# Kept rows stored later, fewer kept combinations, and the first tile's end inside the third stage of a four-layer kernel

## The chip, the cores and the metric

The kernel runs on one core of a Trainium2 chip. The metric is the device time of one execution, in microseconds (us); a run's time is the time of that core.

## What is computed

Four layers act on x of 2048 rows by 640 columns, in float32, each adding its result to x after a layer norm:

```python
x = x + _A_ref(_layernorm(x), A_wqkv, A_wo)
x = x + _B_ref(_layernorm(x), ...)
x = x + _A_ref(_layernorm(x), A_wqkv, A_wo)
x = x + _B_ref(_layernorm(x), ...)
# A: attention, 32 heads of 20, each row sees 8 rows at distances 0, 2, ... 14
# B: a = x @ dft_hid_re.T ; b = x @ dft_hid_im.T
#    y = dft_seq_re @ a - dft_seq_im @ b
```

The change lies in layers B. They are numbered 1 and 3 in the code (`self.li`).

## The kernel before

**Layer B.** Its rows, after the norm, stand in four SBUF tiles `self.xn[0..3]` (shown as `r1_0` to `r1_3`), four rows of blocks each, every value split into a high half and a low half so that three matmul passes of the rounded type give float32 precision (`PASSES`). The sequence matrices come from HBM in pieces of 128 x 512 (`cs_in`, 256 KB), which land in the buffers `win` (a ring of five) and `xa` (two). ScalarE (ACT) makes the high half of a piece and VectorE (DVE) the low half; such a pair is a split. Some pieces are first combined with one another by a DVE addition (line 1536 in layer 3, `combine`).

**Stages.** The eight output tiles are made in three steps. `z_mm` (line 1182) makes the sequence products of tiles 0 and 1 over 16 row blocks; `ymm` (line 1249) multiplies them by the hidden matrices and `yout` adds the old x and stores. Tiles 2 to 7 are then made in three pairs (`p` = 0, 1, 2), each pair in three sweeps (`sw`) of eight steps (`i`), by sums and differences of row blocks that need fewer products. These row combinations (`xc` in HBM) are made by `x_whole` and `x_combine` (line 1799) while `z_mm` still runs. Combination 3 is simply the plain rows, which `x_keep` (line 1299) stores, eight stores of 256 KB. Layer 1 runs the pairs by `pair` (line 1851), layer 3 by `pairs7` (line 1478), which also makes the hidden products with fewer multiplications: `v_stage` (line 1444) does one of eight stages of them for a tile, and needs sums of the hidden matrices (`wvb` in HBM), which `v_get` loads back, so many in each step as the table `GETS` says for each sweep of pair 0.

**Kept combinations.** In the third sweep of a pair, layer 1 forms b11 + b12 of two loaded pieces and stores the result in HBM (`ccb`, `keep`, line 1912, 24 stores of 256 KB); layer 3 loads it (`pre`, line 1511) in place of the plain piece, and so does no addition there.

**What sets the order.** All loads and stores of these stages are issued by SyncE (SP) in one queue. Instructions of each engine run in the order in which they are placed. In `run` (line 2015) only TensorE (PE) keeps the order of the code; the others are placed by a scheduler at build time, `x_keep` among them. In `pairs7` all engines but GpSimd (POOL) keep the order of the code. There, `load(n)` and `loadx(n)` fetch the pieces and row combinations of step n two steps ahead, `fifo` holds the splits to be made, and `fill` makes them as soon as one of six places is free (four in the columns 0 to 255 of `r1_2` and `r1_3`, and `s0`, `s1`); a place comes free when PE has used the half before it.

**The end of tile 1's sequence products.** After the last `z_mm` the five PSUM banks `m0`, `m1`, `xt`, `t0`, `t1` are emptied by `evac1` into `zo0`, `zo1`, `zo2` and `ot`. The first step of `pairs7` writes the same banks again: its first product m0 and m1, its second xt and t0, its third t1 and `pq`.

Of the kernel before, what the change touches and what calls it, by code (L numbers as in the profile page):

```python
# [10 lines left out]
F32 = mybir.dt.float32  # L11
# [139 lines left out]
NP = 8  # L151
# [17 lines left out]
    (2, ("a22", "t4"), (1, 0), (1, 0)),  # L169
    (3, None, (1, 1), (1, 1)),  # L170
)
GETS = ((0, 1, 1, 1, 1, 1, 1, 2), (2, 2, 1, 1, 1, 1, 1, 1), (0, 0, 1, 1, 1, 1, 1, 1))
NST = 16
FA = 64
GW = (512, 512, 512, 384)
SLOTS = NJ + W - 1
# [5 lines left out]
def tile_layers(ctx: ExitStack, tc: tile.TileContext, x, wqkv, wo, cs, cst, wre, wim, out):  # L182
# [897 lines left out]
    class LayerB:  # L1080
# [397 lines left out]
        def pairs7(self):  # L1478
# [32 lines left out]
            def pre(p, i):  # L1511
                tag, bufs = wide[self.nraw % len(wide)]
                self.nraw += 1
                raw = T([P, 2, 256], tag, bufs=bufs) if tag != "win" else wtile([P, 2, 256])
                nc.sync.dma_start(raw.rearrange("p r t -> p (r t)"), ccb[:, p, i])
                return raw

            def load(n):
                if n >= len(steps):
                    return  # L1520
                p, sw, i = steps[n]
                t1, t2 = 2 * p + 2, 2 * p + 3
                if sw == 0:
                    raws[n] = [self.s_raw(*a, wide) for a in ((t1, NP + i), (t1, i), (t2, NP + i))]
                elif sw == 1:
                    raws[n] = [self.s_raw(*a, wide) for a in ((t1, i), (t2, NP + i), (t1, NP + i))]
                else:
                    raws[n] = [self.s_raw(*a, wide) for a in ((t2, NP + i), (t2, i))] + [pre(p, i)]

            def loadx(n):  # L1530
                if n < len(steps):
# [11 lines left out]
            def atoms(n):  # L1543
# [31 lines left out]
                    combine(b22, b12, b22, ALU.subtract)  # L1575
                    half(n, "c3", b22)

                return [c0, lambda: half(n, "p12", raws[n][1]), lambda: half(n, "c6", raws[n][2])]

            fifo = []  # L1580
            held = [0]
# [31 lines left out]
                fifo += atoms(n)  # L1613
            for n in range(2):
                loadx(n)
            for n, (p, sw, i) in enumerate(steps):
                t1, t2 = 2 * p + 2, 2 * p + 3
                tp = t1 - 1
# [180 lines left out]
        def x_combine(self, m, i):  # L1799
            (ca, ka), (cb, kb), sign = XC[m]  # L1800
            op = ALU.add if sign > 0 else ALU.subtract
            va, vb = (self.whole[c][:, :, k * 256 : (k + 1) * 256] for c, k in ((ca, ka), (cb, kb)))
            self.nc_ += 1
            tag = CFG["xcr"][self.nc_ % len(CFG["xcr"])]
            hl = T([P, 2, 2, 256], tag, F32R, bufs=CFG["bufs"].get(tag, 2))
            hi, lo = hl[:, :, 0], hl[:, :, 1]
            nc.vector.tensor_tensor(lo.bitcast(F32), va, vb, op=op)
            nc.scalar.copy(hi, lo.bitcast(F32))
            nc.vector.tensor_tensor(lo, lo.bitcast(F32), hi.bitcast(F32), op=ALU.subtract)
            nc.sync.dma_start(self.xc[m][:, i : i + 2], hl.bitcast(F32))  # L1810

        def x_slot(self, m, i, slots):
            c, j = slots[self.nx % len(slots)]
# [37 lines left out]
        def pair(self, p, nstats, hooks=None):  # L1851
# [63 lines left out]
            def ahead_c(i):  # L1915
                b12, b22, b11 = raw(t2, i), raw(t2, NP + i), raw(t1, i)
                x6 = self.x_slot(6, i, ring)
                c3 = split(combine(b22, b12, b22, ALU.subtract))

                def rest():  # L1920
                    keep(i, combine(b11, b11, b12, ALU.add))
                    return split(b11)

                return x6, c3, split(b12), rest
# [90 lines left out]
        def run(self, nstats):  # L2015
# [6 lines left out]
            with ExitStack() as st:  # L2022
# [3 lines left out]
                for s in range(NST):  # L2026
# [4 lines left out]
                        if f"{t}{s}" not in self.done:  # L2031
                            fn()
                    self.z_mm(s, None, 1)
                    if self.seven and 4 <= s < 4 + NP:
                        self.x_keep(s - 4)
                    self.tick()
                    for h in range(2):
                        ks = [k for k in range(KD) if R["y"][h][k] == s]
# [6 lines left out]
                            fn, args = todo.pop(0)  # L2045
                            fn(*args)
                assert not todo
                if R["y"][1][4] == NST:
                    self.ymm(0, 1, R["y"][1].index(NST), KD)
                    self.yout(0, 1, nstats)  # L2050
                self.evac(1)
            if self.seven:
                with tc.manual_schedule(engines=ENGINES - {nc.gpsimd.engine}):
                    self.pairs7()
# [74 lines left out]
```

## Time and profile before

| what | value |
|---|---|
| three runs | 1736.44, 1732.24, 1733.15 us |
| their median | 1733.15 us |
| the profiled execution's own time | 1733.94 us |
| its span in the trace | 1732.2 us |
| busy time in the span | PE 1709.7, DVE 1383.2, ACT 830.6, POOL 615.2 us |
| granted PE clock | 1.0 throughout, that is the 2.4 GHz level |
| moved by DMA | 444.45 MB, 257 GB/s on average |

The span runs from the first to the last instruction; 1.7 us lie around it. Busy times of the engines overlap. Idle time of PE is what counts here, since PE is busy nearly throughout; an idle time of DVE or ACT costs only where PE waits for it in the end.

### The profile page before, as it was taken

What the parts mean: (1) busy time and instruction counts of PE and PEld (TensorE: products, weight loads), DVE (VectorE), ACT (ScalarE), POOL (GpSimd) and SP (SyncE); (2) the same over time, 40 slices, a digit from 0 to 9 for tenths busy, and PEclk for the clock granted to TensorE, in tenths of its full rate; (3) what the DMA queues carried; (4) which work ended last, traced back from release to release, by engine and by line L of the source; (5) the groups of instructions that cost most, each with busy time, mean ns of one, the idle gap of its engine ahead of it and who ended that gap; (6) DMA issues with size and microseconds to landing.
All of it is one profiled execution on the core that took longest, in us unless ns stands there. A gap on an engine that the chain in (4) does not pass through costs nothing.

```text
span 1732.2 us, 26800 instructions
## 1 busy us (share of the span) xinstructions
PE 1709.7 (99%) x8771; PEld 1487.6 (86%) x8771; DVE 1383.2 (80%) x2201; ACT 830.6 (48%) x1838; POOL 615.2 (36%) x570
## 2 busy tenths in 40 slices
PE   9999999999999999999999999999999999999999
PEld 7888887878888888888888889888888888888888
DVE  5999999978778767767739998899787668778775
ACT  5665645655455445445534444455543444444541
POOL 4899999940000000000019997899300000000000
PEclk9999999999999999999999999999999999999999
DMA  7877679959899788787658856799588988878872
GB/s 253 258 228 260 213 242 312 330 191 353 275 334 303 252 260 262 229 277 242 210 160 271 259 172 212 239 329 331 175 319 294 293 276 271 256 255 266 266 248 88
DMA packets 296059, 444.45 MB, mean 257 GB/s; under 512 B 32080, under 2 KB 171728, under 8 KB 295664
## 3 DMA queue, kind: packets, MB, share of 16 engines
q1 hardware_dynamic: 281744, 433.06, 75.3%
q10 hardware_dynamic: 14176, 9.67, 1.8%
q8 instruction: 70, 1.15, 0.3%
q14 instruction: 69, 0.57, 0.1%
HBM read 345.18 MB, written 97.46 MB: 256 GB/s over the span
## 4 chain that ended last, share of the span: by engine, by line
PE 82%; DVE 7%; DMA 5%; ACT 2%; issue 2%; POOL 2%; SPq 0%; ACTq 0%; DVEq 0%
PE m L513 19%; PE aux L1249 9%; PE aux L676 6%; PE t L1601 5%; PE m L1601 5%; PE m L1843 5%; PE t L1843 5%; PE aux L1465 5%; PE m L1182 4%; PE t L1182 4%; PE pq L1601 3%; PE pq L1843 3%; PE xt L1601 2%; PE xt L1843 2%; DMA win<-cs_in 2%
## 5 line engine op out<-in xcount | busy, mean ns | idle before, releaser
L513 PE MATMUL m<-r,s 128*128 128x512 f32 (+1 forms) x1890 | 421.8, 378 | 0.1
L513 PEld LDWEIGHTS m<-r,s 128*128 128x128 f32 x1890 | 344.6, 188 | 54.6 <-ACT sg L528 1.4
L593 DVE TENSOR_TENSOR pr<-pq,win 128x1280 f32<-128x1280 f32 x128 | 189.8, 1483 | 37.2 <-PE aux L1249 20.3
L651 POOL TENSOR_TENSOR pr<-pr 128x640 f32<-128x640 f32 x126 | 207.7, 1648 | 27.9 <-DVE pr L636 26.6
L596 POOL TENSOR_TENSOR pr<-pr 128x640 f32<-128x640 f32 x123 | 176.7, 1436 | 88.1 <-DVE pr L593 88.0
L636 DVE TENSOR_TENSOR pr<-pq,win 128x1280 f32<-128x1280 f32 x128 | 190.3, 1488 | 2.6
L314 POOL TENSOR_TENSOR stats<-stats,mhalf 128x1 f32<-128x1 f32 (+1 forms) x26 | 18.9, 728 | 448.7 <-ACT stats L308 448.7
L1249 PE MATMUL aux<-r2a,zo 128*128 128x320 f32 x480 | 141.4, 309 | 0.0
L1249 PE MATMUL aux<-pr,zo 128*128 128x320 f32 x440 | 130.1, 309 | 0.0
L652 POOL TENSOR_TENSOR pr<-pr 128x320 f32<-128x320 f32 x126 | 112.9, 896 | 9.9
L606 DVE TENSOR_REDUCE lg<-pr 128x64 f32<-128x640 f32 (+1 forms) x128 | 107.2, 837 | 11.5 <-POOL pr L596 11.2
L1836 ACT CAST r<-win 128x512 fp32r<-128x512 f32 x126 | 76.2, 618 | 75.8 <-DVE win L1872 54.7
L1182 PE MATMUL m<-s,r 128*128 128x512 f32 x348 | 106.9, 395 | 2.4 <-ACT r L1119 0.9
L1182 PE MATMUL t<-s,r 128*128 128x512 f32 x348 | 105.2, 390 | 0.0
L1540 ACT CAST r<-win 128x512 fp32r<-128x512 f32 x111 | 68.3, 621 | 75.4 <-DVE win L1536 34.8
L527 ACT COPY stg<-m 128x480 f32<-128x480 f32 x96 | 53.6, 558 | 94.2 <-PE m L513 88.2
L1837 DVE TENSOR_TENSOR r<-win,r 128x512 fp32r<-128x512 f32 x126 | 84.6, 688 | 16.7 <-ACT r L1836 16.1
L1541 DVE TENSOR_TENSOR r<-win,r 128x512 fp32r<-128x512 f32 x111 | 75.9, 689 | 23.1 <-ACT r L1540 22.9
L1249 PEld LDWEIGHTS aux<-r2a,zo 128*128 128x128 f32 x480 | 90.1, 188 | 1.4
L1249 PEld LDWEIGHTS aux<-pr,zo 128*128 128x128 f32 x440 | 82.6, 188 | 1.6
L676 PE MATMUL aux<-r2a,ot 128*128 128x320 f32 x540 | 83.7, 310 | 0.0
L676 PEld LDWEIGHTS aux<-r2a,ot 128*128 128x128 f32 x540 | 80.4, 188 | 1.5 <-ACT wa L499 0.3
(450 smaller groups left out, 3827.2 us busy)
## 6 DMA issues: line engine op xcount, KB each, us to landing
win<-cs_in SPq DMA_DIRECT2D x330, 256.0 KB
r<-xc SPq DMA_DIRECT2D x264, 256.0 KB
win<-kvb SPq DMA_DIRECT2D x96, 440.0 KB
xa<-cs_in SPq DMA_DIRECT2D x112, 256.0 KB
win<-kvb SPq DMA_DIRECT2D x64, 360.0 KB
xc<-sg SPq DMA_DIRECT2D x28, 512.0 KB
kvb<-stg SPq DMA_DIRECT2D x33, 320.0 KB
qs<-qb SPq DMA_DIRECT2D x64, 160.0 KB
```

Source lines behind the costliest of these rows:

```text
L513: nc.tensor.matmul(mt[g][:, : GW[q]], st[:, a, k], wq[q][:, b, k], start=n == 0, stop=n == 14)
L593: nc.vector.tensor_tensor(pr, q, wview(u, jp, 0, [[1, FE]]), op=ALU.mult)
L596: nc.gpsimd.tensor_tensor(pv[:, :, 0:10], pv[:, :, 0:10], pv[:, :, 10:20], op=ALU.add)
L606: nc.vector.tensor_reduce(rows(lgs[u], jp), pv.rearrange("p (a h) d -> p a h d", h=HE), axis=AX.X, op=ALU.add,)
L636: nc.vector.tensor_tensor(pr.rearrange("p j w (h d) -> p (j w) h d", d=DH), rows(lgs[u], jp).unsqueeze(3).to_broadcast([P, 2 * W, HE, DH]) ...
L651: g.tensor_tensor(pr[:, :, 0:4], pr[:, :, 0:4], pr[:, :, 4:8], op=ALU.add)
L652: g.tensor_tensor(pr[:, :, 0:2], pr[:, :, 0:2], pr[:, :, 2:4], op=ALU.add)
L676: nc.tensor.matmul(m[:, :320], oT[(c, j)][:, a, k], wo_s["w"][:, b, k, e * 320 : (e + 1) * 320], start=(i, k) == (0, 0), stop=(i, k) == (2 ...
L1182: self.last = nc.tensor.matmul(self.z[t][k], self.xn[c][:, a, j, k * P : (k + 1) * P], self.ct[s][:, b], start=s == 0 and i == 0, stop=s = ...
L1249: self.last = nc.tensor.matmul(self.ym[e][:, :320], zt[(k, a, ri)][:, j2 * P : (j2 + 1) * P], w[:, e * 320 : (e + 1) * 320], start=(k, a, ...
L1601: nc.tensor.matmul(bank, w(a, kb), h[b], start=start and (a, b) == (0, 0) and not cont, stop=stop and (a, b) == (1, 0), skip_group_check=cont,
L1843: nc.tensor.matmul(bank, w(a, kb), hl[b], start=start and (a, b) == (0, 0), stop=stop and (a, b) == (1, 0),)
```

## The change

Five things are done:

- Layer 1 no longer stores the combinations of pair 2 for steps 4 to 7 (`kept`), 4 stores of the 24. Layer 3 loads the plain piece for these steps and adds it itself on DVE.
- `x_keep` is called in the last eight rounds of `z_mm` in place of rounds 4 to 11, and each of its stores is put behind the last store of `x_combine` on SP (`issue_after`).
- In layer 3, the last `ymm`, the emptying of tile 1's banks and the last `yout` leave `run` and stand at the start of `pairs7`, behind the loads of the first two steps; a split is made ahead of the emptying and another behind the third bank. So DVE and ACT now keep the written order there.
- In `GETS`, the third sweep's loads of sums stand one step earlier each: counts 0, 1, 1, 1, 1, 1, 1, 0 in place of 0, 0, 1, 1, 1, 1, 1, 1.
- `keep` is split so that the addition is done in any case.

```diff
-GETS = ((0, 1, 1, 1, 1, 1, 1, 2), (2, 2, 1, 1, 1, 1, 1, 1), (0, 0, 1, 1, 1, 1, 1, 1))
+GETS = ((0, 1, 1, 1, 1, 1, 1, 2), (2, 2, 1, 1, 1, 1, 1, 1), (0, 1, 1, 1, 1, 1, 1, 0))
+def kept(p, i):
+    return p < NPAIR - 1 or i < NP // 2
...
-                    raws[n] = [self.s_raw(*a, wide) for a in ((t2, NP + i), (t2, i))] + [pre(p, i)]
+                    raws[n] = [self.s_raw(*a, wide) for a in ((t2, NP + i), (t2, i))]
+                    raws[n].append(pre(p, i) if kept(p, i) else self.s_raw(t1, i, wide))
...
-                return [c0, lambda: half(n, "p12", raws[n][1]), lambda: half(n, "c6", raws[n][2])]
+                def c2():
+                    _, b12, b11 = raws[n]
+                    if not kept(p, i):
+                        combine(b11, b11, b12, ALU.add)
+                    half(n, "c6", b11)
+
+                return [c0, lambda: half(n, "p12", raws[n][1]), c2]
...
             for n in range(2):
                 loadx(n)
+            if self.y1 < KD:
+                self.ymm(0, 1, self.y1, KD)
+            self.zt_new(1)
+            fill(1)
+            for k in range(KD):
+                self.evac1(1, k)
+                if k == 2:
+                    fill(1)
+            if self.y1 < KD:
+                self.yout(0, 1, None, 2)
...
-            nc.sync.dma_start(self.xc[m][:, i : i + 2], hl.bitcast(F32))
+            self.sdma = nc.sync.dma_start(self.xc[m][:, i : i + 2], hl.bitcast(F32))
...
-                    keep(i, combine(b11, b11, b12, ALU.add))
+                    combine(b11, b11, b12, ALU.add)
+                    if kept(p, i):
+                        keep(i, b11)
...
-                    if self.seven and 4 <= s < 4 + NP:
-                        self.x_keep(s - 4)
+                    if self.seven and s >= NST - NP:
+                        with tc.issue_after(self.sdma.ins):
+                            self.x_keep(s - NST + NP)
...
-                if R["y"][1][4] == NST:
-                    self.ymm(0, 1, R["y"][1].index(NST), KD)
-                    self.yout(0, 1, nstats)
-                self.evac(1)
+                self.y1 = R["y"][1].index(NST) if R["y"][1][4] == NST else KD
+                if not self.seven:
+                    if self.y1 < KD:
+                        self.ymm(0, 1, self.y1, KD)
+                        self.yout(0, 1, nstats)
+                    self.evac(1)
```

PE's instructions, and POOL's, are the same ones in the same order in both kernels. DVE has four additions more, in layer 3, and SP four stores less, in layer 1.

**SP at the end of layer 1's pair 2, before.** Lines 1826 and 1816 load pieces and row combinations, line 1913 stores the kept combination from the buffer in which it was made.

```order
L1913 DMA ccb_131<-win_1195_8409 128x512
L1826 DMA win_1201_8461<-cs_in 128x512
L1826 DMA win_1203_8506<-cs_in 128x512
L1816 DMA r1_1_544_3397<-xc_0_6_123 128x2x256
L1826 DMA win_1204_8508<-cs_in 128x512
L1826 DMA win_1205_8510<-cs_in 128x512
L1913 DMA ccb_131<-win_1201_8461 128x512
L1826 DMA win_1211_8564<-cs_in 128x512
L1816 DMA r1_1_544_3397<-xc_0_6_123 128x2x256
L1826 DMA win_1212_8566<-cs_in 128x512
L1913 DMA ccb_131<-win_1205_8510 128x512
L1826 DMA win_1213_8568<-cs_in 128x512
```

The same place with the change (1849 and 1839 are the same loads):

```order
L1849 DMA win_1201_8460<-cs_in 128x512
L1849 DMA win_1203_8504<-cs_in 128x512
L1849 DMA win_1204_8506<-cs_in 128x512
L1839 DMA r1_1_544_3397<-xc_0_6_123 128x2x256
L1849 DMA win_1205_8508<-cs_in 128x512
L1849 DMA win_1211_8561<-cs_in 128x512
L1839 DMA r1_1_544_3397<-xc_0_6_123 128x2x256
L1849 DMA win_1212_8563<-cs_in 128x512
L1849 DMA win_1213_8565<-cs_in 128x512
L341 DMA xa_1206_8546<-xs_1_0_146 128x640
L355 DMA win_1224_8649<-wqkv_in 128x512
```

The three stores of steps 5 to 7 that stood among these loads are gone, and a load no longer stands behind a store of the buffer that it reuses.

**DVE at the end of tile 1 in layer 3, before.** Lines 1225 and 1228 empty banks, 1541 makes a low half, 1536 combines, 1262 adds the old x into `xr`.

```order
L1228 TENSOR_TENSOR zo1_1916_13381<-m1_1848_12793,zo0_1915_13380 128x256
L1228 TENSOR_TENSOR zo1_1916_13381<-m1_1848_12793,zo1_1916_13381 128x256
L1536 TENSOR_TENSOR win_1927_13413<-win_1927_13413,xa_1925_13409 128x512
L1225 TENSOR_TENSOR zo2_1917_13382<-xt_1849_12794,zo1_1916_13381 128x512
L1228 TENSOR_TENSOR zo2_1917_13382<-t0_1850_12795,zo2_1917_13382 128x256
L1541 TENSOR_TENSOR s0_1931_13439<-win_1926_13411,s0_1931_13439 128x512
L1262 TENSOR_TENSOR xr_1914_13375<-aux0_1902_13223,xr_1914_13375 128x320
L1541 TENSOR_TENSOR s1_1932_13442<-win_1927_13413,s1_1932_13442 128x512
L1536 TENSOR_TENSOR win_1929_13421<-win_1928_13419,win_1929_13421 128x512
L1262 TENSOR_TENSOR xr_1914_13375<-aux1_1903_13224,xr_1914_13375 128x320
L1228 TENSOR_TENSOR ot_1918_13383<-t0_1850_12795,zo2_1917_13382 128x256
L1225 TENSOR_TENSOR ot_1918_13383<-t1_1851_12796,ot_1918_13383 128x512
```

The same place with the change (1231 and 1234 empty banks, 1548 makes a low half, 1543 combines, 1268 adds):

```order
L1231 TENSOR_TENSOR zo0_1923_13393<-m0_1847_12788,zo0_1923_13393 128x512
L1234 TENSOR_TENSOR zo1_1924_13394<-m1_1848_12789,zo0_1923_13393 128x256
L1234 TENSOR_TENSOR zo1_1924_13394<-m1_1848_12789,zo1_1924_13394 128x256
L1231 TENSOR_TENSOR zo2_1925_13395<-xt_1849_12790,zo1_1924_13394 128x512
L1543 TENSOR_TENSOR win_1919_13369<-win_1919_13369,win_1917_13365 128x512
L1548 TENSOR_TENSOR r1_2_1750_12134<-xa_1918_13367,r1_2_1750_12134 128x2x256
L1234 TENSOR_TENSOR zo2_1925_13395<-t0_1850_12791,zo2_1925_13395 128x256
L1234 TENSOR_TENSOR ot_1926_13396<-t0_1850_12791,zo2_1925_13395 128x256
L1231 TENSOR_TENSOR ot_1926_13396<-t1_1851_12792,ot_1926_13396 128x512
L1268 TENSOR_TENSOR xr_1927_13416<-aux0_1902_13215,xr_1927_13416 128x320
L1268 TENSOR_TENSOR xr_1927_13416<-aux1_1903_13216,xr_1927_13416 128x320
L1548 TENSOR_TENSOR r1_3_1803_12484<-win_1919_13369,r1_3_1803_12484 128x2x256
```

The two rows on `ot` stood behind two low halves of `s0` and `s1`, a combination and both additions into `xr`; now they stand right behind the emptying of t0, and the low half of the first step's third product (`r1_3` from `win_1919`) stands behind them and behind the additions.

**SP ahead of the first steps of `pairs7`, before.** Line 1810 stores row combinations, 1816 loads them back for a step, 1826 loads pieces.

```order
L1810 DMA xc_1_2_126<-stg_1899_13197 128x1024
L1810 DMA xc_1_5_124<-sg3_1893_13145 128x1024
L1826 DMA win_1926_13411<-cs_in 128x512
L1810 DMA xc_1_7_125<-sg3_1898_13192 128x1024
L1826 DMA win_1927_13413<-cs_in 128x512
L1816 DMA r1_0_1608_11204<-xc_1_5_124 128x2x256
L1816 DMA r1_0_1608_11204<-xc_1_7_125 128x2x256
L1816 DMA r1_1_1715_11859<-xc_1_5_124 128x2x256
L1816 DMA r1_1_1715_11859<-xc_1_7_125 128x2x256
L1826 DMA win_1928_13419<-cs_in 128x512
L1810 DMA xc_1_1_127<-sg3_1904_13237 128x1024
L1826 DMA win_1929_13421<-cs_in 128x512
```

The same place with the change (1833 stores, 1307 is `x_keep`, 1839 and 1849 load, 341 loads the old x for `yout`):

```order
L1833 DMA xc_1_2_126<-stg_1899_13189 128x1024
L1833 DMA xc_1_5_124<-sg3_1893_13137 128x1024
L1307 DMA xc_1_3_129<-r1_0_1608_11200 128x2x256 x3
L1849 DMA win_1921_13373<-cs_in 128x512
L1833 DMA xc_1_7_125<-sg3_1898_13184 128x1024
L1849 DMA win_1922_13375<-cs_in 128x512
L1839 DMA r1_0_1608_11200<-xc_1_5_124 128x2x256
L1833 DMA xc_1_1_127<-sg3_1904_13229 128x1024
L1839 DMA r1_0_1608_11200<-xc_1_7_125 128x2x256
L1839 DMA r1_1_1715_11855<-xc_1_5_124 128x2x256
L1839 DMA r1_1_1715_11855<-xc_1_7_125 128x2x256
L341 DMA xr_1927_13416<-xs_2_0_150 128x640
```

Three stores of kept rows now stand ahead of the pieces and rows of the first steps (one stands earlier still), four more follow behind the last combination, ahead of the second step's next pieces, and the load of the old x stands behind the first rows where it stood ahead of all these.

## Rows read from the trace of the kernel before

**Rows 1.** The page's first part: busy us, share of the span, instructions.
```profile
PE 1709.7 (99%) x8771; PEld 1487.6 (86%) x8771; DVE 1383.2 (80%) x2201; ACT 830.6 (48%) x1838; POOL 615.2 (36%) x570
```

**Rows 2.** Waits of PE, whole kernel: us in total, times, longest.
```profile
PE pq L365 <- DVE s L376: 2.2, 2, 1.2
PE aux L476 <- DVE r L292: 1.8, 1, 1.8
```

**Rows 3.** Timeline of SP, end of layer 1's pair 2: start us, length us.
```profile
829.05 0.33 SPq L1913 DMA_DIRECT2D ccb<-win  x1
...
831.98 0.33 SPq L1826 DMA_DIRECT2D win<-cs_in  x1
```

**Rows 4.** Timeline of DVE, same place: start, length, in brackets idle before.
```profile
836.01 0.69 DVE L1872 TENSOR_TENSOR win<-win,win 128x512 f32<-128x512 f32 x1 [2.25 <-DMA win<-cs_in]
...
837.26 0.69 DVE L1872 TENSOR_TENSOR win<-win,win 128x512 f32<-128x512 f32 x1
...
838.48 0.42 DVE L376 TENSOR_TENSOR s<-pq,s 128x256 fp32r<-128x256 f32 x1
```

**Rows 5.** Windows: stretch, length, busy us (x) of PE, PEld, DVE, ACT, POOL, PEclk, DMA share, GB/s.
```profile
1312.00:1324.00 12.00, 11.33 (x55) 9.36 (x54) 11.21 (x22) 6.29 (x12) 0.00 (x0) 1.00 0.62 202
...
1340.00:1344.00 4.00, 4.00 (x20) 3.30 (x19) 3.46 (x6) 2.03 (x5) 0.00 (x0) 1.00 1.08 352
```

**Rows 6.** Timeline of PE, end of the third layer.
```profile
1146.49 0.73 PE L1182 MATMUL m<-s,r 128*128 128x512 f32 x2 [0.75 <-DMA s<-c0b]
...
1160.25 2.03 PE L676 MATMUL aux<-r2a,s 128*128 128x320 f32 x12 [1.08 <-DVE r L292]
```

**Rows 7.** Timeline of DVE, pair 2, third sweep, step 4: last low half.
```profile
1682.39 0.68 DVE L1541 TENSOR_TENSOR r<-xa,r 128x512 fp32r<-128x512 f32 x1
```

**Rows 8.** Timeline of PE, the product that uses it.
```profile
1684.37 1.52 PE L1601 MATMUL m<-r,r 128*128 128x512 f32 x6
```

**Rows 9.** View of line 1301 (`x_keep`): ns min/median/max, first and last start us.
```profile
L1301 SPq DMA_DIRECT2D xc<-r x8: 365/370/425, 1104.3 to 1182.0; - x8
```

**Rows 10.** Timeline of DVE, pair 0, sweep 1, step 6 of 0 to 7.
```profile
1337.88 0.69 DVE L1541 TENSOR_TENSOR r<-win,r 128x512 fp32r<-128x512 f32 x1 [0.73 <-ACT r L1540]
```

**Rows 11.** Timeline of PE, the same step's first product.
```profile
1340.53 1.52 PE L1601 MATMUL m<-r,r 128*128 128x512 f32 x6
```

**Rows 12.** Timeline of PE, second product of the first step.
```profile
1317.99 0.93 PE L1601 MATMUL t<-r 128*128 128x512 f32 x3 [0.67 <-DVE ot L1228]
```

**Rows 13.** Timeline of DVE, emptying of tile 1's banks.
```profile
1313.89 0.68 DVE L1225 TENSOR_TENSOR zo<-xt,zo 128x512 fp32r<-128x512 f32 x1
...
1317.43 0.42 DVE L1228 TENSOR_TENSOR ot<-t,zo 128x256 fp32r<-128x256 f32 x1
```

**Rows 14.** Timeline of SP, a load of the third step.
```profile
1305.20 0.33 SPq L1826 DMA_DIRECT2D xa<-cs_in  x1
```

**Rows 15.** Chain that ended last, two of its pieces: start us, us from issue to landing.
```profile
1314.00 2.39 DMA xa<-cs_in
...
1545.63 5.84 DMA r<-xc
```

**Rows 16.** Timeline of PE, third sweep of pair 0: step 4, then its end.
```profile
1418.12 0.93 PE L1601 MATMUL xt<-r,r 128*128 128x512 f32 x3
...
1443.07 0.56 PE L1465 MATMUL aux<-r2a,zo 128*128 128x320 f32 x2 [1.22 <-DMA r2a<-wvb]
1443.98 1.30 PE L1465 MATMUL aux<-r,zo 128*128 128x320 f32 x7 [0.35 <-DVE qs L1474]
```

**Rows 17.** Timeline of SP, pair 0, third sweep: row loads, last two loads of sums.
```profile
1412.11 0.91 SPq L1816 DMA_DIRECT2D r<-xc  x2
...
1433.42 0.46 SPq L1355 DMA_DIRECT2D r2a<-wvb  x1
...
1437.34 0.33 SPq L1355 DMA_DIRECT2D r2a<-wvb  x1
```

**Rows 18.** Timeline of DVE, the end of that sweep.
```profile
1443.44 0.48 DVE L1474 TENSOR_TENSOR qs<-aux,qs 128x320 f32<-128x320 f32 x1
```

## The prediction

> **Bound.** I read the page first: PE is busy 1709.7 us [rows 1] of a span of 1732.2 us, so all idle time of PE together is 22.5 us. An edit that takes no matmul away can only win part of that, and the diff takes none away. Then the waits of PE: no single one is longer than 1.8 us [rows 2]. So the question is which of these small waits lie where the change works, what stands right behind each of them, and what new wait the moved transfers and vector instructions could make. For that I read the timelines at five places, the view of one line, the windows, and two pieces of the chain that ended last, which show how long a load takes from issue to landing.
>
> **Part 1.** *Four stores less in layer 1.* A kept combination is stored from the buffer in which it was made, and the buffer is not free before the store has read it. In steps 4 to 7 of pair 2 the store at 829.05 is followed by a load that goes out at 831.98 [rows 3]. That load is late for DVE: the last step's combination waits 2.25 us for it, the next one stands at 837.26, and behind both, at 838.48, stands the DVE instruction that PE needs for its next transposes [rows 4]; it ends at 838.90, and PE's longest wait on it is 1.2 us [rows 2]. Without the stores the buffer is free as soon as DVE has read it. Two stores of 256 KB also leave the way of the last loads: at 352 GB/s, what DMA moves where it is saturated [rows 5], one takes 262144 / 352000 = 0.74 us. Two of them are 1.5 us, more than the wait, so the wait can go in full: the gain lies between 0 and 1.2 us. It must last to the end. At 1160.25 PE waits 1.08 us for DVE [rows 6], and DVE is there behind its own chain of attention products; if that chain does not come sooner, PE only waits longer. I take 0.8 us.
>
> **Part 2.** *Four additions more in layer 3.* One is 0.69 us [rows 4], and the piece is now loaded from another matrix with the same 256 KB. DVE makes it ahead of the step's last low half. In pair 2's step 4 that half ends at 1682.39 + 0.68 = 1683.07, and its product starts at 1684.37 [rows 7, 8]: 1.30 us of cover, 0.61 us with the addition in front. So it costs 0. Were the cover gone it would cost 0.69 us in a step, 2.8 us in four.
>
> **Part 3.** *Kept rows stored later.* Eight issues of 0.37 us go from 1104 to 1182 us [rows 9] to the end of the row combinations, and with them 8 x 0.74 = 5.9 us of transfers. At the old place a load makes PE wait 0.75 us at 1146.49 [rows 6], but the next wait, at 1160.25, is DVE's: PE would come to it 0.75 us sooner and wait 0.75 us longer. I take 0, with 0 to 0.75 us of gain as bounds. At the new place seven of the eight stand ahead of loads of the first steps of `pairs7`. They need 5.2 us of DMA time. From 1312 to 1324 DMA moves 202 GB/s where 352 are possible [rows 5]: (352 - 202) x 12 us = 1.8 MB, or 5.1 us of room. So the stores just fit. Behind that, DMA is saturated, and the tightest step I found there is step 6: its low half ends at 1338.57, PE starts on it at 1340.53 [rows 10, 11], 1.96 us of margin. Part 4 lets PE come 0.67 us sooner, which leaves 1.29 us. I take 0; the cost if the room isn't there is the second rival.
>
> **Part 4.** *The end of the first tile.* PE waits 0.67 us at 1317.99 for the second half of bank t0 [rows 12], which DVE empties at 1317.43, long after it has emptied xt at 1313.89 [rows 13]; between them stood work for later steps. By the new order, even if xt is emptied no sooner than now (ends 1314.57), there follow one combination and one low half (0.69 each) and the two halves of t0 (0.42 each): 1316.8 at the latest. PE comes there at 1317.99 - 0.67 = 1317.32, so this wait goes. What is late next is the low half of the third product, which now stands behind the emptying of t1 (0.69) and both additions of the old x (0.49 each, estimated from the 320 columns against the 0.69 of 512): at the latest 1316.8 + 0.69 + 0.98 + 0.69 = 1319.2. But two instructions of 0.69 that stood ahead of xt have gone behind it, so I expect 1317.8, and PE needs it in its second matmul of that product, about 1318.2. So the gain is 0.67 us, and the bounds are 0.67 us of gain and 0.3 us of loss (1319.2 against 1318.2, less 0.67).
> The third step's load that went out at 1305.20 [rows 14] now waits for the buffer that the second product's low half frees, 1315.95 at the latest, and lands 2.39 us later [rows 15], at 1318.3. Steps follow each other by some 4.1 us (1340.53 less 1317.99 over five and a half steps), so that step starts near 1323.5: no wait.
>
> **Part 5.** *Sums one step ahead.* PE waits 1.22 us at 1443.07 for the last of six loads of sums [rows 16], issued at 1437.34; its place is now that of the load at 1433.42 [rows 17], 3.9 us sooner. So that wait goes. It isn't a gain: PE's next stage starts at 1443.98 and waits for DVE's `qs`, which runs 1443.44 to 1443.92 [rows 16, 18] and does not depend on the sums. PE would merely come to it sooner. And one more load of 160 KB (0.47 us at 352 GB/s) now stands ahead of everything that this sweep loads. In the fifth step PE starts at 1418.12 on rows that were asked for at 1412.11 [rows 16, 17]; the load of the same step in pair 1 takes 5.84 us [rows 15], so these land near 1418, with no margin, and may come up to 0.47 us later. The splits ahead of `qs` wait for loads of the same queue. I take 0.3 us of loss, between 0.47 of loss and 1.2 of gain.
> The row shows 5.84 us from issue to landing for 256 KB. The Trainium skill's page DMA: Bandwidth & Descriptors (section Anatomy of one DMA, fitted on another issuing path) gives about 2.0 us and the bytes at 436 GB/s, an estimate of 2.6 us. By that the rows would have come 3.4 us ahead of use, part 5 would lose nothing and the sum would be 0.3 us lower; the trace's 5.84 us decides.
>
> **The sum.** -0.8 + 0 + 0 - 0.67 + 0.3 = -1.2 us. The profiled execution took 1733.94 us, 0.8 us over the median of the runs; with the change it would take 1732.7, and the median goes from 1733.15 to 1732.0 us.
>
> **Rivals.** *Every wait is paid back in full.* The waits touched are 1.2, 0.75, 0.67 and 1.22 us; all of them gone is 3.8 us, 1729.3 us. For it: each is a wait of PE, and PE is the bound. Against it: behind two of them stands a wait for DVE (1160.25 and 1443.98) that the change doesn't touch. The Trainium skill's page Perfetto Trace Analysis (section Optimization Strategy) advises finding the gaps of the bounding engine and making what they wait for start sooner, which leads to this result.
> *The stores collide with the first sweep.* If the room from 1312 to 1324 isn't there, since loads now wait for buffers in it (part 4), the 5.2 us of stores push the loads of the saturated stretch back. It decides from 1.29 us of lateness on, and each further us costs one. All 5.2 us late cost 3.9 us, and with part 5's 0.47 in full and part 1 as taken the time is 1733.15 + 3.9 - 0.67 - 0.8 + 0.47 = 1736.1 us, slower than before. For it: DMA share 1.08 [rows 5] behind that place. Against it: the room just suffices.
> *The reordering moves the wait and doesn't remove it.* The third product's low half, or the old x landing late for the additions in front of it, holds PE at the first step as long as t0 did. Then part 4 is between 0 and 0.3 of loss: 1733.15 - 0.8 + 0.3 + 0.1 = 1732.8 us.
>
> **Numbers.** 0.58 for the sum as worked out (1730.6 to 1733.0), 0.12 for the first rival, 0.17 for the second, 0.13 for the third. The likeliest gives 1732.0 us. The range takes in both bounds of part 5 and the first two rivals, and the runs of before, which lie 0.9 under and 3.3 us over their median: 1729.0 to 1736.5. About 0.3% (5.2 us) is what a measurement of this kernel can tell from no change. Faster by more needs over 5.2 us out of waits that add up to 3.8: 0.03. Slower by more needs the second rival at its full price and a wait that I haven't seen besides: 0.06. Within: 0.91.
>
> **Signs.** Right: PE's wait for the transposes in layer 1 well under 1.2 us; none for `ot` at the first step of `pairs7`; none for `r2a`, but a longer one for `qs` in its place, and one of some tenths for `r<-xc` in step 4 of pair 0's third sweep. Wrong: PE waiting for low halves in steps 4 to 7 of the first sweep (second rival), for `r` at the first step's third product (third), or starting the stage behind `qs` a full 1.2 us sooner relative to the sweep (first). A PE idle sum that fell by more than 4 us, or rose at a place where nothing was moved, would mean that I misread what the change touches.

## The result and the profile after

The changed kernel took 1736.98 us (median of 22 runs, 1734.62 to 1742.66), the kernel before, run beside it, 1734.66 (22 runs, 1730.12 to 1737.37). The ratio is 1.0018 with a 95% interval of 1.001 to 1.0026: the change costs 3.1 us (1.7 to 4.5). That is within 0.3%, but on the other side of what was predicted, and 1736.98 lies above the range. Of the distance to the forecast 1.5 us are the kernel before itself, which took 1734.66 us here and 1733.15 in the three runs that the forecast started from: 1733.15 times the ratio is 1736.3 us, inside the range. What has to be explained is the direction. The profiled execution took 1739.04 us, with a span of 1737.3 against 1732.2 before.

First the busy times on the page of the changed kernel; they answer to [rows 1]:

```profile
PE 1713.0 (99%) x8771; PEld 1487.3 (86%) x8771; DVE 1384.9 (80%) x2205; ACT 830.2 (48%) x1838; POOL 615.2 (35%) x570
```

DVE has four instructions more. PE runs the same 8771 matmuls and its idle time grew only from 22.5 to 24.3 us. The other 3.3 us are in the busy time, because a stall shows only partly as a wait. An example from the changed kernel:

```profile
1685.09 0.50 PE L1614 MATMUL m<-r,r 128*128 128x512 f32 x1
1685.81 1.45 PE L1614 MATMUL m<-r,r 128*128 128x512 f32 x5 [0.23 <-DVE r L1548]
```

The two starts lie 0.72 us apart. Where nothing stalls, such matmuls follow each other every 0.23 us (six from 1681.39 to 1682.75). So 0.49 us are lost, and the bracket shows 0.23. For the size of a loss I therefore read distances between two starts of PE, not sums of waits.

Second the waits of PE in the changed kernel, over the whole span (us in total, times, longest); they answer to [rows 2]:

```profile
PE aux L1471 <- DVE qs L1480: 2.7, 2, 1.9
...
PE pq L371 <- DVE s L382: 1.3, 2, 0.9
```

The waits for the transposes in layer 1 fell from 2.2 to 1.3 us. At the top stands a wait for `qs` that occurs twice. One was expected, behind pair 0's third sweep. The other is new, and so is all else in the same view from 1675 us to the end, where the view of the kernel before lists no wait of PE:

```profile
PE aux L1471 <- DVE qs L1480: 0.8, 1, 0.8
PE aux L1471 <- DVE s L1480: 0.5, 1, 0.5
PE m L1614 <- DVE r L1548: 0.4, 2, 0.2
PE m L1614 <- ACT r L1547: 0.3, 1, 0.3
PE xt L1614 <- DVE r L1548: 0.2, 1, 0.2
```

This is pair 2's third sweep with the four new additions, the part that I had costed at nothing. The distance from the last product of step 3 to the matmuls `aux<-pr,zo` of the sums behind the sweep measures it. PE's timeline of the changed kernel:

```profile
1681.39 1.52 PE L1614 MATMUL m<-s,r 128*128 128x512 f32 x6
...
1712.54 1.59 PE L1471 MATMUL aux<-pr,zo 128*128 128x320 f32 x9 [0.51 <-DVE s L1480]
```

and of the kernel before:

```profile
1680.92 1.52 PE L1601 MATMUL m<-s,r 128*128 128x512 f32 x6
...
1707.41 1.48 PE L1465 MATMUL aux<-pr,zo 128*128 128x320 f32 x9
```

31.15 us against 26.49: 4.66 us are lost in this stretch alone. The rest of the kernel took 0.4 us more than before by the span of the two profiled executions (5.1 in all), and by the ratio of all runs about 1.6 us less (3.1 less 4.66). What an addition does there is seen on DVE, step 4, changed kernel:

```profile
1680.84 0.69 DVE L1543 TENSOR_TENSOR xa<-win,xa 128x512 f32<-128x512 f32 x1 [1.66 <-DMA win<-cs_in]
1682.35 0.69 DVE L1548 TENSOR_TENSOR r<-xa,r 128x512 fp32r<-128x512 f32 x1 [0.82 <-ACT r L1547]
1682.96 0.69 DVE L1548 TENSOR_TENSOR r<-win,r 128x512 fp32r<-128x512 f32 x1
1683.56 0.69 DVE L1543 TENSOR_TENSOR xa<-xa,win 128x512 f32<-128x512 f32 x1
1685.07 0.69 DVE L1548 TENSOR_TENSOR r<-xa,r 128x512 fp32r<-128x512 f32 x1 [0.82 <-ACT r L1547]
...
1691.61 0.69 DVE L1548 TENSOR_TENSOR s<-win,s 128x512 fp32r<-128x512 f32 x1 [0.82 <-ACT s L1547]
...
1704.72 0.69 DVE L1548 TENSOR_TENSOR s<-win,s 128x512 fp32r<-128x512 f32 x1 [0.82 <-ACT s L1547]
```

The fourth line is the addition. Its own place is 0.6 us, but the low half behind it starts 1.51 us after it (1685.07 less 1683.56): it needs the high half, which ACT can only make once the sum is there, and DVE runs nothing else meanwhile. ACT's timeline shows the instruction:

```profile
1684.41 0.62 ACT L1547 CAST r<-xa 128x512 fp32r<-128x512 f32 x1 [1.58 <-DVE xa L1543]
```

From the addition's end (1683.56 + 0.69 = 1684.25) it is 0.16 us to ACT, 0.62 us of ACT, 0.04 us back: the 0.82 us in brackets. Without the addition ACT makes this half in a row with the others, and DVE goes on without a wait. ACT in the kernel before, the same step:

```profile
1681.05 0.62 ACT L1540 CAST r<-win 128x512 fp32r<-128x512 f32 x1
1681.57 0.62 ACT L1540 CAST r<-xa 128x512 fp32r<-128x512 f32 x1
```

and DVE there; the last low half, [rows 7], follows 0.60 us behind the second:

```profile
1681.18 0.69 DVE L1541 TENSOR_TENSOR r<-xa,r 128x512 fp32r<-128x512 f32 x1 [0.82 <-ACT r L1540]
1681.79 0.69 DVE L1541 TENSOR_TENSOR r<-win,r 128x512 fp32r<-128x512 f32 x1
```

So the low half moves by 1.51 us, not by 0.60.

### The profile page after: what moved, and what is told of

It is laid out like the page before. It is cut to its first block, busy times and chain, and to the rows that moved or that the text cites. A ratio compares the mean times of both kernels' runs of the same rounds, so it can differ in the third digit from the quotient of the medians.

```text
span 1737.3 us, 26799 instructions
## 1 busy us (share of the span) xinstructions
PE 1713.0 (99%) x8771; PEld 1487.3 (86%) x8771; DVE 1384.9 (80%) x2205; ACT 830.2 (48%) x1838; POOL 615.2 (35%) x570
## 4 chain that ended last, share of the span: by engine, by line
PE 74%; DVE 11%; DMA 7%; issue 3%; ACT 2%; POOL 2%; SPq 0%; ACTq 0%; DVEq 0%
PE m L519 19%; PE aux L1255 8%; PE aux L682 6%; PE m L1614 5%; PE t L1614 5%; PE aux L1471 4%; DMA win<-cs_in 4%; PE m L1866 4%; PE t L1866 4%; PE m L1188 3%; PE t L1188 3%; PE pq L1614 3%; PE xt L1614 2%; PE xt L1866 2%; PE pq L1866 2%
## 5 line engine op out<-in xcount | busy, mean ns | idle before, releaser
L657 POOL TENSOR_TENSOR pr<-pr 128x640 f32<-128x640 f32 x126 | 207.8, 1649 | 26.9 <-DVE pr L642 25.7
```

Source lines behind the costliest of these rows:

```text
L657: g.tensor_tensor(pr[:, :, 0:4], pr[:, :, 0:4], pr[:, :, 4:8], op=ALU.add)
```

## Experiments

The theories. **A**: the four late additions cost 4.6 us, not by DVE's time but by the second trip from DVE to ACT and back; the rest of the change gains. **B**: the piece's new source lands later. **C**: the moved stores, the new order of the first tile's end, or the loads of sums make the loss. **D**: DVE's own 0.6 to 0.69 us per addition.

In the table, "us" is the ratio less one, times 1735, and "stretch" the distance between the two starts of PE shown above. The stretch is from one profiled execution each. Each ratio is to the kernel before as it ran beside that kernel (medians 1733.92 us for e1 to e4, 1735.20 for e5 to e8, 1736.25 for e9 to e12).

| kernel | ratio (95% interval) | us | stretch, us |
|---|---|---|---|
| before | 1 | 0 | 1680.92 to 1707.41: 26.49 |
| changed | 1.0018 (1.001 to 1.0026) | +3.1 | 1681.39 to 1712.54: 31.15 |
| e1 all kept | 0.9989 (0.9979 to 0.9999) | -1.9 | 1677.87 to 1704.31: 26.44 |
| e2 kept only | 1.002 (1.001 to 1.003) | +3.5 | 1681.15 to 1711.16: 30.01 |
| e3 no addition | 0.999 (0.998 to 1.0001) | -1.7 | 1682.77 to 1709.68: 26.91 |
| e4 early addition | 0.9992 (0.9981 to 1.0004) | -1.4 | 1680.53 to 1707.21: 26.68 |
| e5 kept only, early | 1.0002 (0.9989 to 1.0014) | +0.3 | 1682.33 to 1708.78: 26.45 |
| e6 e4, old stores | 0.9997 (0.9985 to 1.001) | -0.5 | 1680.65 to 1707.76: 27.11 |
| e7 e4, old loads of sums | 0.9978 (0.9966 to 0.999) | -3.8 | 1680.56 to 1707.00: 26.44 |
| e8 e4, old tile end | 0.9985 (0.9972 to 0.9998) | -2.6 | 1680.29 to 1706.91: 26.62 |
| e9 none kept, early, old loads | 0.9973 (0.9963 to 0.9982) | -4.7 | 1677.16 to 1704.13: 26.97 |
| e10 all kept, old loads | 0.9994 (0.9986 to 1.0003) | -1.0 | 1682.65 to 1709.12: 26.47 |
| e11 eight late additions | 1.0033 (1.002 to 1.0045) | +5.7 | 1682.70 to 1715.15: 32.45 |
| e12 e4, sums two steps ahead | 0.9989 (0.9979 to 1.0) | -1.9 | 1678.18 to 1704.62: 26.44 |

**e1 and e2: the change cut in two.** e1 is the changed kernel with all combinations kept, so it holds parts 3 to 5 alone; e2 is the kernel before with parts 1 and 2 alone (`kept`, its use in layer 1, and `c2` as in the change).

```diff
 def kept(p, i):
-    return p < NPAIR - 1 or i < NP // 2
+    return True
```

> The changed kernel, but all combinations kept again (eight stores in each pair of layer 1, no addition in layer 3). Theory A (the four additions in layer 3 cost 4.6 us of PE waits in pair 2's third sweep and the end behind it; the rest of the change wins 1.6 us, 0.8 of it by the four stores left out): 0.8 us under before, no PE wait in the third product's code between 1680 and 1700 us, and the wait of about 1.2 us for the transposes near 839 us back. Rival C (the moved stores, the new order of the first tile's end and the sums' loads make the loss): still 3 to 4 us over before.

> The kernel before with this part of the change alone: in pair 2 only steps 0 to 3 keep their combinations, steps 4 to 7 add in layer 3. Theory A: 4.6 of loss in layer 3 less 0.8 of gain in layer 1, 3.8 us over before. Rival C: 0 to 0.8 us under before.

e1 came 1.9 us under before, e2 3.5 us over. C falls: the moved work alone does not lose. The stretch carries the loss where the late additions are and nowhere else. One thing in e1's expectation missed: PE's wait for the transposes near 839 us did not come back, though the four stores did. PE's timeline of e1 shows this place and two others:

```profile
693.07 1.20 PE L1866 MATMUL m<-r,r 128*128 128x512 f32 x4 [1.35 <-DVE r L1860]
...
839.98 0.49 PE L371 MATMUL pq<-ident,xa 128*128 128x128 f32 x3
...
847.03 0.44 PE L371 MATMUL pq<-ident,xa 128*128 128x128 f32 x2 [1.16 <-DVE s L382]
```

PE had already waited 1.35 us at 693 us, at a product that the change does not touch, and came to the transposes 2.3 us later than before (839.98 us against 838.95 less a wait of 1.24), late enough to find them ready. Before, there was no such wait at 693. So the wait at 839 is no safe measure of what the stores cost.

**e3 and e4: addition or landing, time or trip.** e3 leaves the addition out; e4 puts it behind the step's first combination:

```diff
 def c0():
-    b22, b12, _ = raws[n]
+    b22, b12, b11 = raws[n]
     combine(b22, b12, b22, ALU.subtract)
+    if not kept(p, i):
+        combine(b11, b11, b12, ALU.add)
     half(n, "c3", b22)
...
 def c2():
-    _, b12, b11 = raws[n]
-    if not kept(p, i):
-        combine(b11, b11, b12, ALU.add)
-    half(n, "c6", b11)
+    half(n, "c6", raws[n][2])
```

> The changed kernel without the four additions in layer 3: the same pieces are loaded from the same matrix, but the sixth product of steps 4 to 7 of pair 2 uses the plain piece, so this part of the sum is left out of the result. Theory A (the addition, and the trip from DVE to ACT and back that it starts): 1.6 us under before, no PE wait at the third sweep's products. Rival B (the piece's new source lands later than the kept one, and that makes PE wait): 2 to 3 us over before, with the waits still there. Rival C: 3 to 4 us over before.

> The changed kernel with the addition at another place: right behind the step's first combination, ahead of its low half, where DVE now stands idle for 0.82 us until ACT has made the high half. Theory A (it is not DVE's 0.6 us but the second trip from DVE to ACT and back, 1.5 us in a step, that costs): within 0.7 us of the kernel without the additions, 1.0 to 1.6 us under before. Rival D (DVE's own time of 0.6 to 0.69 us in a step is what costs): it stays near the changed kernel, 2 to 3 us over before. Rival B, too: 2 to 3 us over before.

By the ratios e3 lies 1.7 us and e4 1.4 us under before. Both intervals (-3.5 to +0.2 and -3.3 to +0.7) include no change and exclude the 2 us and more over before that B and D ask for. Their stretches are back at 26.9 and 26.7 us. B falls with e3: the pieces come from the new source there too, and one wait of 0.2 us is all that is left of PE's waits. D falls with e4: the same four additions are made and the loss is gone. DVE in e4: the last low half of step 4, then step 5 from its two additions on, then the last low half of step 7:

```profile
1682.68 0.69 DVE L1548 TENSOR_TENSOR r<-xa,r 128x512 fp32r<-128x512 f32 x1
...
1685.00 1.28 DVE L1543 TENSOR_TENSOR win<-win,win 128x512 f32<-128x512 f32 x2
1686.51 0.69 DVE L1548 TENSOR_TENSOR r<-win,r 128x512 fp32r<-128x512 f32 x1 [0.22 <-ACT r L1547]
1687.11 1.29 DVE L1548 TENSOR_TENSOR s<-win,s 128x512 fp32r<-128x512 f32 x2
...
1697.64 0.68 DVE L1548 TENSOR_TENSOR s<-win,s 128x512 fp32r<-128x512 f32 x1
```

The addition is the second of the "x2" at 1685.00. The idle time before the first low half fell from 0.82 to 0.22 us: the addition lies in it, and the three low halves then run without a gap. The early addition needs its piece sooner: in e4 DVE waited 1.31 us for it ahead of step 4's addition, and such a wait (0.47 to 1.96 us) stands in five of the seven kernels that add early. PE's view from 1675 us on lists no wait in any of the seven. From step 4 to step 7 DVE takes (1697.64 less 1682.68) / 3 = 4.99 us a step, in the changed kernel (1704.72 less 1685.07) / 3 = 6.55. In between, no wait of DVE in the changed kernel is for a load; all are for ACT. PE takes 5.91 in e4, from the same products' starts:

```profile
1684.17 1.52 PE L1613 MATMUL m<-r,r 128*128 128x512 f32 x6
...
1701.90 1.52 PE L1613 MATMUL m<-s,r 128*128 128x512 f32 x6
```

So the late addition makes DVE with its trips to ACT slower than PE in these four steps. The lag lasts to the end of the sweep, where DVE has to empty the banks before PE can go on: in the changed kernel that work starts at 1706.33 us, 1.61 us after the start of the last low half, with DVE busy without a gap from there to `qs`:

```profile
1706.33 0.68 DVE L1543 TENSOR_TENSOR stg<-xt,stg 128x512 f32<-128x512 f32 x1
...
1709.91 0.48 DVE L1480 TENSOR_TENSOR qs<-aux,qs 128x320 f32<-128x320 f32 x1
```

PE waits 0.8 us for that `qs`. In e4 the same first emptying stood at 1700.73 and itself waited 0.20 us for PE. The Trainium skill's page Trainium Architecture — The Big Picture (section Inside one NeuronCore) says that each engine has its own instruction stream and that they synchronize only through semaphores. The rows agree: in each 0.82 us in which DVE waits for ACT, it runs none of the instructions that stand behind that wait.

**e11: more late additions**, in all eight steps of pair 2.

```diff
-    return p < NPAIR - 1 or i < NP // 2
+    return p < NPAIR - 1
```

> The changed kernel with the late addition in all eight steps of pair 2's third sweep (eight stores less in layer 1). Theory A (each late addition takes 1.5 us of DVE's chain, against 2.7 to 12 us of cover in steps 0 to 3): more than the changed kernel, 3.5 to 6 us over before, with waits from step 2 or 3 on. Rival (the loss belongs to the later landing of step 4's loads, not to the number of additions): 3 us over before, as with four.

It came 5.7 us over before, and the stretch grew by another 1.30 us, to 32.45. The waits that were expected from step 2 or 3 on begin only at step 4 (1684.96 us). The four added steps cost less than the last four: ahead of step 4 DVE stood idle for 1.66 us in the changed kernel, and in e11 it has no idle time at this place, so that this slack takes up part of the lag. Step 4's first combination on DVE, in e2 and in e11; in the changed kernel it is the row at 1680.84 above:

```profile
1679.47 0.69 DVE L1543 TENSOR_TENSOR xa<-win,xa 128x512 f32<-128x512 f32 x1 [0.53 <-DMA win<-cs_in]
...
1683.44 0.68 DVE L1543 TENSOR_TENSOR xa<-win,xa 128x512 f32<-128x512 f32 x1
```

From this start to the second start of PE in the table it is 31.69 us in e2, 31.70 in the changed kernel and 31.71 in e11. So in all three the end of the stretch hangs on DVE's chain from step 4 on, and they differ by when this chain begins: 1.68 us ahead of the start of the stretch in e2, 0.55 us ahead of it in the changed kernel, 0.74 us behind it in e11. The waits of PE from 1675 us on are those of the changed kernel, that for `xt` twice, and a new one (lines 1, 2 and 3 of the view):

```profile
PE aux L1471 <- DVE qs L1480: 0.8, 1, 0.8
PE aux L1471 <- DVE s L1480: 0.5, 1, 0.5
PE xt L1614 <- ACT r L1547: 0.5, 1, 0.5
```

**e5: parts 1 and 2 with the early addition, on the kernel before.**

> The kernel before with the first part of the change alone (pair 2 keeps only steps 0 to 3), and the four additions in DVE's idle time behind the step's first combination. Theory A: nothing lost in layer 3, the gain in layer 1 left: 0.8 us under before (0 to 1.4). If the four stores less win nothing in layer 1: within 0.3 us of before.

It came 0.3 us over before (-1.9 to +2.4). The stretch has no loss (26.45 us), but no gain of the four stores shows; 0.8 us is not excluded.

**e6, e7, e8, e10, e12: parts 3 to 5 one by one.** On e4, e6 takes back the stores' place, e7 the loads' steps, and e8 the place of the first tile's end (the ten lines ahead of the loop of `pairs7` go, and `run` ends as before). The edits of e6 and e7:

```diff
-                    if self.seven and s >= NST - NP:
-                        with tc.issue_after(self.sdma.ins):
-                            self.x_keep(s - NST + NP)
+                    if self.seven and 4 <= s < 4 + NP:
+                        self.x_keep(s - 4)
...
-GETS = (..., (0, 1, 1, 1, 1, 1, 1, 0))
+GETS = (..., (0, 0, 1, 1, 1, 1, 1, 1))
```

e12 puts `(1, 1, 1, 1, 1, 1, 0, 0)` there, and e10 makes e7's edit on e1.

> The kernel with the early addition (1.4 us under before), with the kept rows stored at their old place again. Theory (this move wins and loses about the same: a wait of 0.5 to 0.9 us for c0b goes, one for DVE near 1291 us and one of 0.4 us near 1341 us come): again 1.4 us under before, within 0.5 us. Rival (the moved stores cost: the waits near 1291 and 1341 us are theirs): 2.5 us under before, with these waits gone. Rival (the move wins): 0.2 us under before.

> The kernel with the early addition, with the loads of the sums at their old steps. Theory (the wait for r2a only takes another name, as the wait for qs): again 1.4 us under before, within 0.5 us, the r2a wait of about 1.2 us back near 1443 us and the one for qs down to 0.3 to 0.4 us. If the earlier load is a gain: 0.2 us under before.

> The kernel with the early addition, with the end of the first tile again ahead of the third stage's first splits. Theory (this part wins the 0.67 us of PE's wait for the second half of t0): 0.7 us under before, the wait back near 1318 us. If the wait only moves to later loads: 1.4 us under before.

> The changed kernel with all combinations kept, and the sums' loads at their old steps. If the earlier loads of sums cost the 2.4 us by which the two kernels with the early addition differ: 4.5 us under before. If that was scatter and the waits only change their names: 2.1 us under before, as with the new loads.

> The kernel with the early addition, with the sums loaded two steps ahead of their old place instead of one. If the earlier loads cost time by standing ahead of the sweep's own loads: more than with one step, 0 to 2 us over before, with PE waiting for r<-xc in pair 0's third sweep. If the place of these loads doesn't matter: 1.4 us under before.

By the times none of the three parts can be told from nothing: all intervals overlap e4's. e7, 2.4 us under e4, looked like a gain from the old loads, but the same edit on e1 gave 0.9 us the other way (e10), and loading still earlier cost nothing (e12). Several of these forecasts missed: e7 (-3.8) and e8 (-2.6) lie lower than any of their values, e6 (-0.5) between two of its three, and e10 (-1.0) short of both of its own. The values lay 0.7 to 2.4 us apart, and the intervals of these times are 3 to 5 us wide. The waits say more. For the sums, PE's timeline at the end of pair 0's third sweep, changed kernel:

```profile
1444.48 1.30 PE L1471 MATMUL aux<-r,zo 128*128 128x320 f32 x7 [1.85 <-DVE qs L1480]
```

and in e12:

```profile
1441.15 1.30 PE L1471 MATMUL aux<-r,zo 128*128 128x320 f32 x7 [0.58 <-DVE qs L1480]
```

With the new loads the wait for `r2a` never occurs. The wait for `qs` that took its place lies between 0.28 and 1.90 us in the eight kernels that have them, 0.94 us in the mean; with the old loads (six kernels) both waits together lie between nothing listed and 1.57, in the mean 0.8 us. A wait for the rows `r<-xc` in step 4 of that sweep, which part 5 feared, stands in two of the eight (e6 1.54 us, e11 0.86) and in one of the six (e5 0.46). For the tile's end, e8 has the old wait of [rows 12] again:

```profile
1318.92 0.93 PE L1613 MATMUL t<-r 128*128 128x512 f32 x3 [0.67 <-DVE ot L1234]
```

It stands, at 0.67 us each time, in all four kernels with the old order (before, e2, e5, e8) and in none of the ten with the new one. For the stores, the old wait for `c0b` near 1146 us [rows 6] stands in all four kernels with the stores at the old place (before, e2, e5, e6: 0.43 to 0.75 us) and in two of the ten with the new place (e4 0.84, e7 0.34). A wait of PE in the last products ahead of `pairs7`, here in the changed kernel, came in:

```profile
1291.06 0.74 PE L1188 MATMUL m<-s,r 128*128 128x512 f32 x2 [0.86 <-DVE s L1171]
```

It is there with 0.2 to 0.9 us in six of ten kernels with the stores at the new place, and is listed in none of the four at the old one (before, e2, e5, e6). DVE's timeline of the changed kernel has a wait of 1.07 us for the store of a combination, `xc<-sg`, five instructions ahead of what PE needs; before it was 0.60 us:

```profile
1286.24 0.69 DVE L1830 TENSOR_TENSOR sg<-s,s 128x512 f32<-128x512 f32 x1 [1.07 <-DMA xc<-sg]
```

That a moved store delays this one fits the rows, but is not shown.

**e9: the early addition everywhere, a version that beats both.** Nothing is kept in layer 1 (`kept` returns `False`), all 24 steps of the third sweeps add early, and the loads of sums stand at their old steps.

> The early addition in all 24 steps of the third sweeps (nothing kept in layer 1, so 24 stores less), and the sums' loads at their old steps. If an addition in DVE's idle time is free everywhere: as the kernel that has it in four steps and the old loads of sums, 3.8 us under before, or up to 1 us better. If pairs 0 and 1 have no such idle time: 0.6 us of DVE in each of 16 steps more, up to 6 us over before.

It took 4.7 us less than before (3.1 to 6.4); its ratio is 0.0045 under the changed kernel's. The page's line, and what it wrote to memory:

```profile
PE 1709.1 (99%) x8771; PEld 1488.1 (86%) x8771; DVE 1396.7 (81%) x2225; ACT 830.1 (48%) x1838; POOL 615.2 (36%) x570
...
HBM read 345.18 MB, written 91.17 MB: 252 GB/s over the span
```

DVE makes 24 instructions more than before and is busy 13.5 us longer, and PE waits for none of it: it has no wait at a product (line 1613) in any of the three pairs, and from 1675 us on no wait at all. 6.3 MB less are written than the 97.46 MB of before, which are the 24 stores of 262144 bytes. e10 tells how much of the 4.7 us goes with them: it has the same parts 3 and 4 and the same loads of sums, ran beside the same kernel before, and differs from e9 only in that it keeps all combinations and adds none. It lies 1.0 us under before, and the two intervals do not overlap (0.9963 to 0.9982 and 0.9986 to 1.0003). So 3.7 us by the ratios, 2.4 by the medians (1731.43 against 1733.79), come with leaving out all 24 stores, although four of them showed nothing in e5. Where in the kernel these microseconds come from was not traced.

## Why the prediction was wrong

**Part 2 is the step that failed.** It said that an addition is 0.69 us, that step 4 has 1.30 us of cover [rows 7, 8], and so that it costs 0, or 2.8 us if the cover goes; the sum has it with 0. Measured: 3.52 us in the stretch of e2, 4.66 in that of the changed kernel. Three things were wrong. The price: 1.51 us, not 0.69, because the low half right behind the addition waits for ACT, and ACT for the sum. The price could be read before: each first combination of a step in this sweep already had 0.82 us of idle time behind it (1681.18 above), as [rows 10] show 0.73 us in another sweep. At 1.51 us one addition is more than the 1.30 us of cover. The cover: it was read from one step as if each step began anew, but DVE's pace went from 4.99 to 6.55 us a step past PE's 5.91, so the lag adds up. And the end: banks to be emptied stand behind the sweep on the same engine. The changed kernel's further 1.1 us over e2 are the later start of step 4 on DVE (0.55 against 1.68 us ahead of the start of the stretch): there DVE waited 1.66 us for a load, against 0.53 in e2 and 0.94 before. The load was asked for as early as before (1676.19 us, 5.20 us ahead of the start of the stretch; before 1675.74, 5.18 ahead) and landed later. Why is not shown. By itself it costs little: e3, with the same wait at 1.86 us and no addition, lost 0.4 us.

**Part 1** (0.8 us of gain). The first half of the reasoning holds: DVE's wait for the load of the last steps' combinations is 1.98 to 2.28 us in the three kernels with all stores (before, e1, e10) and at most 1.45 us in the eleven that leave at least four out. The second half, that PE gains by it, is not shown. The wait at 839 did shrink from 1.24 to 0.41 us in the changed kernel, as the sign said, but not because DVE was sooner there:

```profile
836.44 0.69 DVE L1895 TENSOR_TENSOR win<-win,win 128x512 f32<-128x512 f32 x1 [1.30 <-DMA win<-cs_in]
...
839.46 0.42 DVE L382 TENSOR_TENSOR s<-pq,s 128x256 fp32r<-128x256 f32 x1
```

The instruction that PE needs stands at 839.46, before at 838.48 [rows 4]; PE came later still, having waited 1.08 us at 692 us. And e1 and e10, which have all the stores, list no wait there. The premise that PE's wait at 1160 us takes such a gain back fails too:

```profile
1159.92 4.66 PE L682 MATMUL aux<-r2a,s 128*128 128x320 f32 x30 [1.09 <-DVE r L298]
```

This wait is 1.07 to 1.10 us in all fourteen kernels, while PE comes to it at anything from 1156.5 to 1163.7 us. What DVE does there follows PE's own work, so the wait moves with PE and takes nothing back.

**Part 3** (0, and the second rival). Right in size as far as the times tell. The collision that the rival feared is a wait of 0.17 us at [rows 11]'s place (1341.18 us), not 3.9. A wait where I had not looked, at 1291 us, came instead. The wait at 1146 us went in eight of the ten kernels with the new place, the changed kernel among them, and the wait at 1160 us did not grow by it. So the reason for taking no gain was wrong there, and if the term came out near 0, it was by luck: one wait went and another came.

**Part 4** (0.67 us of gain). The wait of [rows 12] went, as worked out, in every kernel with the new order. That this reaches the end can't be seen in times that scatter by more, and e8, which has the wait, was no slower than e4 (-2.6 against -1.4 us).

**Part 5** (0.3 us of loss). Right in kind: the wait took another name [rows 16], 0.94 against 0.8 us in the mean. The sign of some tenths for `r<-xc` did not show in the changed kernel, only in e6 and e11; e5 has it with the old loads.

Parts 3 to 5 together, predicted at -0.37 us, measured -1.9 (e1, -3.6 to -0.2). With the addition in its right place the forecast sum would have fitted: -1.2 predicted, -1.4 measured (e4, -3.3 to +0.7). That interval is too wide to confirm the terms, and parts 1 and 3 had reasons that failed, so the near agreement is in part luck. The rivals with a chance spoke of mishaps with stores and loads and of one moved wait; the mechanism that decided was in none of them.

## What to carry to other kernels

An added instruction costs its own time only where the next one on its engine does not need what another engine makes of its result. Otherwise add the wait for the trip there and back, here 0.82 us on top of 0.69. Put it where the engine already stands idle for such a trip: here PE then waited for none of 24 additions. Compare paces per step over the whole loop, not the margin of one step, and look at what the same engine must do right behind the loop.

## What was not expected of the hardware

Kernels with the same code at a place show different waits there: 0 to 2.0 us at the product near 693 us, 0.28 to 1.90 us ahead of the sums in the eight with the new loads. Each has one trace, so whether executions of one kernel differ as much was not tried. One profile against another can't settle a change of 1 us by such a wait. The stretch, measured by itself, can: it stays within 26.4 to 27.1 us in the eleven kernels without late additions and is 30.0 us and more in the three with them.
